# Two tiles' value products in one step, a fourth buffer for transposed weights, and earlier conversion of the values

## The chip, the core and the metric

The kernel runs on one core of one Trainium2 chip. What counts is the time of one execution on the device, in microseconds (us). Lower is better. A measurement of this kernel can tell a change of about 0.3% (3 us) from none.

The engines that matter here are TensorE (PE: matrix products, with its weight loads as PEld), VectorE (DVE), ScalarE (ACT), GpSimd (POOL) and SyncE (SP), whose queue issues most transfers. Each engine works through its own instructions in the order in which the program gives them.

## What is computed

The reference is causal attention with a cumulative bias, followed by two MLPs:

```python
scores = scale * np.matmul(q, k.transpose(0, 1, 3, 2))          # 4 batches, 8 heads, 576 tokens, 64 wide
cum = np.cumsum(np.maximum(s, 0.0), axis=-1)
bias = -(cum[:, :, :, None] - cum[:, :, None, :])
scores = np.where(causal, -1000000000.0, scores + np.minimum(bias, 0.0))
attn = np.exp(scores - np.max(scores, axis=-1, keepdims=True))
attn = attn / (np.sum(attn, axis=-1, keepdims=True) + 1e-09)
x = np.matmul(attn, v)                                          # then (2304 tokens, 512)
h = np.maximum(x @ w_in, 0.0);  x = h * h @ w_out               # first MLP, 2048 wide
h = x @ w_in2;                  y = (h * np.cos(h)) @ w_out2    # second MLP, 2048 wide
```

## The kernel before

The 2304 tokens are cut into nine blocks of 256. Attention is a list of 160 tiles ("jobs"): up to 128 query rows of one head against all keys up to the causal limit. The jobs of a block belong to eight heads of one or two batches, and a head has one or two jobs in a block. Jobs 0 to 31 (the first 16 head units, `n < EARLY`) are done in plain f32. From job 32 on, everything is split into a high and a low part.

`step` emits the program one step at a time, and this is what sets the order on every engine: there is one list of instructions, written step by step. Step i holds, for different jobs, the products of queries and keys (`emit_qk(i)`), the mask and the row minimum of job i - 1 on DVE (`emit_mask`), the exponential on ACT, and the split of job i - 2 into two f16 halves `p` on DVE (`emit_split`), after which SP issues a transposing transfer `pt<-p`. Then come the products with the values (`emit_pv`, "pv" below) of the job that is `lag` steps back: 3 for the early jobs, 5 for the others. One of these is a group of 9, 12 or 15 PE products of 64 columns in f16 (3 or 6 for the shortest tiles). When both heads of a pair are done, the next step evacuates them on DVE (`evacuate`, which writes `xp`), and PE turns `xp` by two f32 transposes into `xps` (`turn`).

Between these lie the slots of the first MLP for the block before: g1 (into `hps`, L844) and g2 (into `y`, L873), 12 products of 256 columns each, in f32r. `slots` is the list of all of them, and each step takes one or two. A block k takes J steps, from the step in which the attention of block k was done (`unit_done`) to the one in which that of block k + 1 is; the last of these J steps has no attention of its own. ACT makes three passes over each g1 result (`gact`: L855, L856, L857), and DVE one (L863).

The values are converted once for every pair of heads (16 conversions): `v_load` on POOL's queue, `v_square` on ACT, a sum over the partitions on PE (`v_sum`, L398), `v_scale` on DVE, `v_high` on ACT, `v_low` on DVE, `v_store` to `v_d` on SP. `vq` holds these by step, and `v_steps` sets the step of each conversion from V_TIME, V_NEAR and V_STRIDE. `load_v` reads a head's part back as `vb`.

The buffers that the change touches: `raw`, `hi` and `k2` (two of each) hold q and k of a head; `pt` has three buffers in turn; `p` has two (a third once the first MLP's weights are converted); `vt` has one and belongs to the conversion of values; all of the pool "at" share the same memory per partition.

After the first MLP come its remaining slots, and the second MLP (L1230 and L1285). The change leaves both alone.

Of the kernel before, what the change touches and what calls it, by code (L numbers as in the profile page):

```python
# [8 lines left out]
F32 = mybir.dt.float32  # L9
F32R = mybir.dt.float32r  # L10
F16 = mybir.dt.float16
# [3 lines left out]
ALU = mybir.AluOpType  # L15
# [9 lines left out]
BT = 256  # L25
# [8 lines left out]
LAG = (3, 5)  # L34
# [45 lines left out]
def _units():  # L80


    out = []
    for k, segs in enumerate(_segments()):
        for b, q0, rws, o in segs:
            nq = sum(rws)
            nk = q0 + nq
            out += [(k, b, h, q0, rws, o, nq, nk, max(nk, 256)) for h in range(H)]
    return out


KQ = 832

WAHEAD = 8
PROLOG_BITS = 0.75

EARLY = 16
# [10 lines left out]
XST_TO = 20  # L108
V_STRIDE = 11
V_NEAR = 6  # L110
V_TIME = 7


@with_exitstack
def attention_moe_moe_kernel(
# [18 lines left out]
    nc = tc.nc  # L134
    ctx.enter_context(tc.manual_schedule())
    heads = _units()

    dram = ctx.enter_context(tc.tile_pool(name="dram", bufs=1, space=DRAM))
    const = ctx.enter_context(tc.tile_pool(name="const", bufs=1))
# [5 lines left out]
    at = at_stack.enter_context(tc.tile_pool(name="at", bufs=1, side="right"))  # L145
# [5 lines left out]

    ext_d = dram.tile([len(heads), 4, KQ], F32, name="ext_d")
    c_d = dram.tile([B * H, 2, S], F32, name="c_d")
# [4 lines left out]
    ident = const.tile([128, 128], F32, name="ident")  # L158
    mask = const.tile([128, 640], BF16, name="mask")

    ones = const.tile([128, 128], F32, name="ones")
    yss = const.tile([128, 2 * NB1], F32, name="yss")
    vsc = const.tile([128, B * H], F32, name="vsc")
    hd, vd, vown = {}, {}, {}
# [29 lines left out]
    for x in range(H // 2):  # L194
        t = wp.tile([128, 2, 2 * BT], F32, tag=f"w{2 * NF - (2, 3, 4, 6)[x]}", name="early")
# [8 lines left out]
    def load_sums(x, eng):  # L204
        nc_ = c8[2 * x:2 * x + 2, 0:BT]
        eng.dma_start(out=early[x][64:65, :, BT:2 * BT], in_=nc_)
        eng.dma_start(out=early[x][65:66, :, 0:BT], in_=nc_)

    def load_raw(n):
        nq, nl = heads[n][6], heads[n][8]  # L210
        if n < H:
            return
        if n < EARLY:
            t = at.tile([128, KQ], F32, tag=("hi", "k2")[n % 2], bufs=2, name="early1")
            nc.sync.dma_start(out=t[0:64, 0:2 * BT], in_=qk[n, 0:64, 0:2 * BT])
            nc.sync.dma_start(out=t[64:66, 0:2 * BT], in_=c1_d[n - H])
            hd[n] = t
            return
        raw = at.tile([128, KQ], F32, tag="raw", bufs=2, name="raw")
        nc.sync.dma_start(out=raw[:, BT - nq:BT + nl], in_=qk[n, :, BT - nq:BT + nl])  # L220
        hd[n] = [None, None, raw]

    def v_own(b):
# [16 lines left out]
    vs = {}  # L240
# [12 lines left out]
    def store_ones(eng, n0, n1):  # L253

        for r in range(2):
            c = slice(BT * r, BT + (KQ - BT) * r)
            eng.dma_start(
# [6 lines left out]
        out=mask[:, 512:640], in_=mask[:, 512:640], pattern=[[-1, 128]], compare_op=ALU.is_ge,  # L264
# [4 lines left out]
        out=ident, in_=ident, pattern=[[-1, 128]], compare_op=ALU.not_equal, fill=1.0,  # L269
# [3 lines left out]
    for t in early[2:]:  # L273
        early_ones(t, nc.gpsimd)
    nc.vector.tensor_scalar(
        out=cs[0:32, 0:S], in0=cs[0:32, 0:S], scalar1=0.0, scalar2=8.0, op0=ALU.max, op1=ALU.mult
    )
    cc = []
    for x0, x1, t in ((0, BT, "xh"), (BT, S, "xl")):
        nc.vector.tensor_tensor_scan(  # L280
            out=c8[0:32, x0:x1], data0=cs[0:32, x0:x1], data1=cs[0:32, x0:x1],
# [5 lines left out]
    for r in range(2):  # L287
        nc.vector.memset(one[0:len(heads), BT * r:BT + (KQ - BT) * r], 1.0 - 2.0 * r)

# [19 lines left out]
    for x in range((XST + 1) // 2):  # L309
        t = wp.tile([128, 2, 512], F32, tag=f"w{2 * NF - 5 - x}", name="xst")  # L310
# [6 lines left out]
    jobs = []  # L317
    last_job = {}
    for n, (u, b, h, q0, rws, o, nq, nk, nl) in enumerate(heads):
        q = q0  # L320
# [12 lines left out]
    def load_ext(n):  # L333
        nq, nl = heads[n][6], heads[n][8]
        if n < EARLY:
            return
        hd[n][0] = at.tile([128, KQ], F32R, tag="hi", bufs=2, name="hi")
        hd[n][1] = at.tile([128, KQ], F32R, tag="k2", bufs=2, name="k2")
        nc.gpsimd.dma_start(out=hd[n][1][64:68, BT - nq:BT + nl], in_=ext_d[n, :, BT - nq:BT + nl])  # L339

    def prep_high(n):
        nq, nk = heads[n][6], heads[n][8]
        if n < EARLY:
            return
        hi, k2, raw = hd[n]
        nc.scalar.copy(hi[:, BT - nq:BT + nk], raw[:, BT - nq:BT + nk])
        nc.scalar.copy(k2[0:64, BT - nq:BT], raw[0:64, BT - nq:BT])

    def prep_low(n):
        nq, nk = heads[n][6], heads[n][8]  # L350
        if n < EARLY:
            return
        hi, k2, raw = hd[n]
        nc.vector.tensor_tensor(
            out=hi[64:128, BT - nq:BT], in0=raw[64:128, BT - nq:BT], in1=hi[64:128, BT - nq:BT], op=ALU.subtract
        )
        nc.vector.tensor_tensor(  # L357
            out=k2[0:64, BT:BT + nk], in0=raw[0:64, BT:BT + nk], in1=hi[0:64, BT:BT + nk], op=ALU.subtract
        )

    def load_v(n):
# [33 lines left out]
    def v_sum(g):  # L395
        n = g[2]
        vs[g]["ps"] = xps[:, BT:BT + n]
        nc.tensor.matmul(vs[g]["ps"], ones, vs[g]["ss"])  # L398

    def v_scale(g):  # L400
        b, h, n, nch = g
# [46 lines left out]
    def v_steps(gs, start):  # L448

        at, due = [], len(jobs) + V_TIME  # L450
        for b, h, n, nch in reversed(gs):
            first = next(
                i for i, j in enumerate(jobs) if j[0] >= 2 * H and heads[j[0]][1] == b and h <= heads[j[0]][2] < h + n
            )
            due = min(first - start + 3 - V_TIME, due - V_NEAR)
            at.insert(0, due)
# [6 lines left out]
    def v_add(gs, at, stored=True):  # L463

        for g, t in zip(gs, at):
            fs = []
            if g not in vs:
                fs, t = [(t, v_load)], t + 2
            fs += [(t, v_square), (t + 1, v_sum), (t + 2, v_scale), (t + 2, v_high), (t + 3, v_low)]
            for x, f in fs + [(t + 3, v_store)] * stored:  # L470
                vq.extend([] for _ in range(x + 1 - len(vq)))
                vq[x].append((f, g))

# [2 lines left out]
    def emit_qk(i):  # L476
        n, ti, q, r = jobs[i]
        u, b, h, q0, rws, o, nq, nk, nl = heads[n]
        if h % 2 == 0 and ti == 0:
            pd[n] = dict(z=at.tile([128, len(rws), 2], F32, tag="z", bufs=5, name="z", padded_shape=[128, 2, 2]))  # L480
        w = q + r
        segs = [(0, 288), (288, 288)] if w > 512 else [(0, max(w, 256))]
        qo = BT - nq + q - q0
        if n < EARLY:
            p = psa.tile([128, 512], F32, tag=f"qk{flip[0]}", bufs=1, name="qkp")
            flip[0] = (flip[0] + 1) % 3
            nc.tensor.matmul(p[0:r, 0:w], hd[n][0:66, qo:qo + r], hd[n][0:66, BT:BT + w])  # L487
            jd[i] = dict(ps=[(p, 0, w)], w=w)
            return
        hi, k2 = hd[n][0], hd[n][1]  # L490
        ps = []
        for k, (c0, cn) in enumerate(segs):
            p = psa.tile([128, 512], F32, tag=f"qk{flip[0]}", bufs=1, name="qkp")
            flip[0] = (flip[0] + 1) % 3
            for m, kk in ((hi, 128), (k2, 68)):
                nc.tensor.matmul(  # L496
                    p[0:r, 0:cn], m[0:kk, qo:qo + r], m[0:kk, BT + c0:BT + c0 + cn],
                    start=(kk == 128), stop=(kk == 68),
                )
            ps.append((p, c0, min(cn, w - c0)))  # L500
        jd[i] = dict(ps=ps, w=w)
# [16 lines left out]
    def p_tile(i):  # L518
        third = nw[2] >= 2 * NF and not wrest and i % 3 == 2
        return at.tile([128, 1280], F16, tag="p3" if third else "p", bufs=1 if third else 2, name="p")  # L520
# [19 lines left out]
    def emit_split(i):  # L540
        n, ti, q, r = jobs[i]
        j = jd[i]
        w, sb = j["w"], j["sb"]
        cw = 128 * ((w + 127) // 128)
        if n < EARLY:
            pp = j["ps"][0][0][:, BT:BT + cw]
            pt = at.tile([128, 640], F32, tag="pt", bufs=3, name="pt1")
            (nc.scalar.copy if ti else nc.vector.tensor_copy)(pt[:, 0:w], pp)
            j["pt"] = pt
            yield  # L550
            return
        p = p_tile(i)
        if cw > w:
            nc.gpsimd.memset(p[0:r, 0:2 * cw].rearrange("p (a c) -> p a c", a=2)[:, :, w:cw], 0.0)
        nc.vector.tensor_scalar(
            out=p[0:r, 0:w], in0=sb[0:r, 0:w], scalar1=PSC, scalar2=None, op0=ALU.mult
        )
        yield
        nc.vector.scalar_tensor_tensor(  # L559
            out=p[0:r, cw:cw + w], in0=sb[0:r, 0:w], scalar=PSC, in1=p[0:r, 0:w],  # L560
            op0=ALU.mult, op1=ALU.subtract,
        )
        pt = at.tile([128, 1280], F16, tag="pt", bufs=3, name="pt")
        pt = pt[:, 0:2 * cw // 128 * r].rearrange("p (a r) -> p a r", r=r)
        nc.sync.dma_start_transpose(out=pt, in_=p[0:r, 0:2 * cw])
        j["pt"] = pt
        yield
# [106 lines left out]
    def job(i):  # L674
        return jobs[i] if 0 <= i < NJ else None

    def lag(i):
        return LAG[not job(i) or jobs[i][0] >= EARLY]

    def heads_ahead(i, *fs):  # L680
        if job(i) and jobs[i][1] == 0:
# [301 lines left out]
    def step(moe=0, bits=0, attn=True):  # L983
# [49 lines left out]
        if attn:  # L1033
            heads_ahead(i, (nraw, load_raw, 4))
# [99 lines left out]
    while prog[0] < unit_done(0):  # L1134
        i = prog[0]
        x = i - FIRST_BITS
        step(bits=int((x + 1) * PROLOG_BITS) - int(x * PROLOG_BITS) if x >= 0 else 0)

    for k in range(NB1):
# [8 lines left out]
        for i in range(J):  # L1148
# [24 lines left out]
            n = len(slots) - last - nslots + math.ceil(nslots * (i + 1) / J)  # L1173
# [135 lines left out]
    for i in range(len(steps2) + G2LAG):  # L1309
# [6 lines left out]
        if new:  # L1316
            p, j, f = steps2[i]
# [89 lines left out]
```

## Time and profile before

| what | value |
|---|---|
| three runs | 998.5, 1000.96, 1001.49 us |
| median of them | 1000.96 us |
| the profiled execution's own time | 1003.76 us |
| its span, first to last instruction | 1002.0 us |
| busy, share of the span | PE 96%, PEld 74%, DVE 72%, ACT 65%, POOL 16% |
| chain that ended last | PE 79%, DVE 8%, DMA 6%, ACT 4% |
| mean granted TensorE clock | 0.995 |

The profiled execution is 2.8 us above the median of the three runs. Sums over the trace are made against 1003.76 us.

PE's busy share counts a product from its start to its modelled end, and products overlap, so 96% does not say that PE was at its best. The timeline does: the distance from one product's start to the next is what a product really costs there.

### The profile page before, as it was taken

Reading aid. Unit: us, or ns where it says so; the run is one execution under the profiler, and the core shown is the slowest. Engines: PE = TensorE matmul, PEld = TensorE weight load, DVE = VectorE, ACT = ScalarE, POOL = GpSimd, SP = SyncE. Lnnn points to the kernel's source line nnn. Section 1 sums busy time; section 2 is a strip of 40 time slices with the busy share of each in tenths; the row PEclk is TensorE's granted clock in tenths of the full one; section 3 lists DMA queues with packets and bytes.
Section 4 is the critical chain, followed back from the end, with each engine's and each line's share of the span. In section 5 each row is a group of like instructions: output and inputs, shape, how many; then the busy total and the mean of one; then the engine's idle time right before and its main releaser. Section 6 shows DMA issues by size and latency. Waiting matters only on the chain.

```text
span 1002.0 us, 20487 instructions
## 1 busy us (share of the span) xinstructions
PE 966.9 (96%) x7266; PEld 740.6 (74%) x7266; DVE 723.9 (72%) x1865; ACT 655.5 (65%) x1596; POOL 163.2 (16%) x258
## 2 busy tenths in 40 slices
PE   5999899999999999999999999999999999999998
PEld 4788898899999998999999997444544454444444
DVE  6879788867777897787888267798887545555555
ACT  4789777767777777767776578777766444433433
POOL 2000011111111121111211023330033341000000
PEclk9999999999999999999999999999999999999999
DMA  8955599746887986467898569210000000011001
GB/s 268 292 182 181 118 202 203 170 111 157 196 162 160 178 193 175 109 155 145 192 206 180 188 237 360 95 43 1 1 1 1 0 1 1 0 43 43 23 20 64
DMA packets 150711, 126.65 MB, mean 126 GB/s; under 512 B 108048, under 2 KB 125792, under 8 KB 150608
## 3 DMA queue, kind: packets, MB, share of 16 engines
q1 hardware_dynamic: 146688, 119.05, 46.1%
q0 software_dynamic: 3904, 6.29, 2.5%
q8 instruction: 57, 0.93, 0.4%
q14 instruction: 46, 0.38, 0.1%
q10 hardware_dynamic: 16, 0.01, 0.0%
HBM read 85.25 MB, written 15.81 MB: 101 GB/s over the span
## 4 chain that ended last, share of the span: by engine, by line
PE 79%; DVE 8%; DMA 6%; ACT 4%; issue 2%; SPq 1%; DVEq 0%; ACTq 0%
PE hps L844 18%; PE y L873 18%; PE o L1285 17%; PE hp L1230 17%; PE qkp L496 4%; PE pvs L590 4%; DMA rw<-in_w_dram 3%; DMA raw<-in_qk_dram 1%; PE xps L644 1%; DVE st L716 1%; DVE sb L510 1%; DVE gl L863 1%; DVE wt L737 0%; DVE k L357 0%; SPq L178 0%
## 5 line engine op out<-in xcount | busy, mean ns | idle before, releaser
L844 PE MATMUL hps<-xh,wt 128*128 128x256 f32 x1152 | 241.4, 292 | 4.1 <-ACT g L855 4.0
L873 PE MATMUL y<-gh,wt 128*128 128x256 f32 x1152 | 237.7, 289 | 0.0
L844 PEld LDWEIGHTS hps<-xh,wt 128*128 128x128 f32 x1152 | 191.7, 194 | 7.0 <-ACT g L855 5.5
L873 PEld LDWEIGHTS y<-gh,wt 128*128 128x128 f32 x1152 | 189.9, 192 | 1.3
L1230 PE MATMUL hp<-yh,wt 128*128 128x512 f16 (+1 forms) x640 | 185.9, 358 | 0.0
L1285 PE MATMUL o<-wt,gh 128*128 128x512 f16 x576 | 171.3, 379 | 2.0 <-ACT wt L1300 1.9
L873 PE MATMUL y<-gl,wt 128*128 128x256 f32 x576 | 163.4, 284 | 2.6 <-DVE gl L863 2.6
L844 PE MATMUL hps<-xl,wt 128*128 128x256 f32 x576 | 164.3, 285 | 0.9 <-DVE xl L661 0.9
L1230 PEld LDWEIGHTS <-wt 128*128 128x128 f16 x960 | 92.2, 98 | 93.3
L1242 ACT ACTIVATE a<-hp,hsc 128x512 f32<-128x512 f32 (+1 forms) x80 | 51.4, 643 | 118.6 <-PE hp L1230 117.2
L855 ACT ACTIVATE g<-hps 128x256 f32<-128x256 f32 x144 | 54.6, 379 | 107.7 <-PE hps L844 105.8
L1230 PE MATMUL hp<-yl,wt 128*128 128x512 f16 (+1 forms) x320 | 114.4, 358 | 0.0
L873 PEld LDWEIGHTS y<-gl,wt 128*128 128x128 f32 x576 | 110.6, 192 | 3.7 <-DVE gl L863 3.1
L844 PEld LDWEIGHTS hps<-xl,wt 128*128 128x128 f32 x576 | 111.7, 194 | 1.4 <-DVE xl L661 1.1
L1285 PE MATMUL o<-wt,gl 128*128 128x512 f16 x288 | 109.2, 379 | 0.4 <-DVE gl L1272 0.4
L1243 DVE TENSOR_SCALAR kf<-a 128x512 f32<-128x512 f32 (+1 forms) x80 | 34.5, 431 | 103.8 <-ACT a L1242 103.4
L1285 PEld LDWEIGHTS <-gh 128*128 128x128 f16 x576 | 56.2, 98 | 66.7 <-issue 2.4
L527 ACT ACTIVATE sb<-sb,nb 128x128 f32<-128x128 f32 (+8 forms) x160 | 93.7, 586 | 12.1 <-DVE nb L510 12.0
L339 POOL DMA_DIRECT2D k<-ext_d x80 | 40.8, 510 | 341.9 <-ACT g L856 92.3
L510 DVE CUSTOM_DVE_ANT_0 sb<-qkp,mask 128x128 f32<-128x128 f32 (+8 forms) x160 | 72.7, 454 | 13.8 <-PE qkp L487 8.6
L1251 ACT ACTIVATE a<-kf 128x512 f32<-128x512 f32 (+1 forms) x80 | 46.8, 585 | 46.6 <-DVE kf L1244 46.1
L559 DVE SCALAR_TENSOR_TENSOR p<-sb,p 128x512 f16<-128x512 f32 (+7 forms) x128 | 72.4, 565 | 4.0
(119 smaller groups left out, 1680.1 us busy)
## 6 DMA issues: line engine op xcount, KB each, us to landing
rw<-in_w_dram SPq DMA_DIRECT2D x64, 512.0 KB
raw<-in_qk_dram SPq DMA_DIRECT2D x32, 352.0 KB
raw<-in_qk_dram SPq DMA_DIRECT2D x16, 384.0 KB
v_d<-vt SPq DMA_DIRECT2D x16, 320.0 KB
raw<-in_qk_dram SPq DMA_DIRECT2D x16, 320.0 KB
vb<-v_d SPq DMA_DIRECT2D x32, 160.0 KB
vr<-in_v_dram POOLq DMA_DIRECT2D x15, 320.0 KB, 4.7
y_d<-yst SPq DMA_DIRECT2D x18, 256.0 KB
```

The lines of the kernel that those rows point to most:

```text
L339: nc.gpsimd.dma_start(out=hd[n][1][64:68, BT - nq:BT + nl], in_=ext_d[n, :, BT - nq:BT + nl])
L496: nc.tensor.matmul(p[0:r, 0:cn], m[0:kk, qo:qo + r], m[0:kk, BT + c0:BT + c0 + cn], start=(kk == 128), stop=(kk == 68),)
L510: nc.vector.tensor_tensor_reduce(out=sb[0:r, c0:c0 + cn], in0=p[0:r, 0:cn], in1=mask[0:r, mo + c0:mo + c0 + cn], scale=-0.125, scalar=(3.0 ...
L527: nc.scalar.activation(out=sb[0:r, 0:w], in_=sb[0:r, 0:w], func=ACTF.Exp, scale=-1.0, bias=j["nb"], accum_out=pd[n - h % 2]["z"][0:r, ti, ...
L559: nc.vector.scalar_tensor_tensor(out=p[0:r, cw:cw + w], in0=sb[0:r, 0:w], scalar=PSC, in1=p[0:r, 0:w], op0=ALU.mult, op1=ALU.subtract,)
L844: nc.tensor.matmul(hp, w[:, a, c * 128:(c + 1) * 128], (xh, xl)[e][:, c, :], start=(n == 0), stop=(n == 3 * KD - 1),)
L855: nc.scalar.activation(out=g, in_=hp, func=ACTF.Relu)
L873: nc.tensor.matmul(yps[k][d // 2][:, d % 2, :], w[:, a, d * 128:(d + 1) * 128], (gh, gl)[e], start=(f == 0 and n == 0 and d % 2 == 0), sto ...
L1230: nc.tensor.matmul(hp, w[:, a, c * 128:(c + 1) * 128], (yh, yl)[e][:, c, :], start=(m == 0), stop=(m == 3 * KD - 1),)
L1242: nc.scalar.activation(out=a, in_=hp, func=ACTF.Copy, scale=sm["hsc"][:, j, f:f + 1], bias=0.25)
L1251: nc.scalar.activation(out=a, in_=kf, func=ACTF.Sin, scale=-6.2831850)
L1285: nc.tensor.matmul(ops[j][a], (gh, gl)[e][:, a * 128:(a + 1) * 128], w[:, x, :], start=(first and m == 0), stop=(last and m == 2),)
```

## The change

In the late part of attention (jobs from 32 on), `lag` becomes 4 for every odd job and stays 5 for every even one. An even job j and the odd job j + 1 then both have their products with the values in step j + 5, and the steps between have none. `unit_done` takes the odd job's lag, so it comes one step earlier for every block from 2 on.

A job whose number is 3 modulo 4 takes its transposed weights into a buffer of its own: `pt4` (1024 columns), or, where it needs more, the buffer of `vt`. The other three of each four jobs share the three `pt` buffers as before.

Memory for `pt4` comes from `raw`, `hi`, `k2` and the early heads' tiles, which have 768 columns in place of 832 (`qb(n)` is where the keys start: 256, or 192 for a head with 576 keys), and from `ones`, which is one column and is broadcast where it is used.

V_TIME goes from 7 to 10, so each conversion of values starts up to three steps sooner; inside a conversion, the sum on PE and all that follows it come one step later than they did after the squares.

```diff
-V_TIME = 7
+V_TIME = 10
...
-    ones = const.tile([128, 128], F32, name="ones")
+    ones = const.tile([128, 1], F32, name="ones")
...
+    def qb(n):
+        return min(BT, SQ - heads[n][8])
...
-        raw = at.tile([128, KQ], F32, tag="raw", bufs=2, name="raw")
-        nc.sync.dma_start(out=raw[:, BT - nq:BT + nl], in_=qk[n, :, BT - nq:BT + nl])
+        raw = at.tile([128, SQ], F32, tag="raw", bufs=2, name="raw")
+        nc.sync.dma_start(out=raw[:, qb(n) - nq:qb(n) + nl], in_=qk[n, :, BT - nq:BT + nl])
...
-        nc.tensor.matmul(vs[g]["ps"], ones, vs[g]["ss"])
+        nc.tensor.matmul(vs[g]["ps"], ones.to_broadcast([128, 128]), vs[g]["ss"])
...
-            fs += [(t, v_square), (t + 1, v_sum), (t + 2, v_scale), (t + 2, v_high), (t + 3, v_low)]
-            for x, f in fs + [(t + 3, v_store)] * stored:
+            fs += [(t, v_square), (t + 2, v_sum), (t + 3, v_scale), (t + 3, v_high), (t + 4, v_low)]
+            for x, f in fs + [(t + 4, v_store)] * stored:
...
-        pt = at.tile([128, 1280], F16, tag="pt", bufs=3, name="pt")
+        if i % 4 < 3:
+            pt = at.tile([128, 1280], F16, tag="pt", bufs=3, name="pt")
+        elif cw * r <= 512 * 128:
+            pt = at.tile([128, 1024], F16, tag="pt4", bufs=1, name="pt4")
+        else:
+            pt = at.tile([128, 1280], F16, tag="vt", bufs=1, name="pt5")
...
     def lag(i):
-        return LAG[not job(i) or jobs[i][0] >= EARLY]
+        if job(i) and jobs[i][0] < EARLY:
+            return LAG[0]
+        return LAG[1] - (i % 2 if job(i) else 0)
```

The lines of the changed kernel lie up to 11 further down than those before (L590 is L599 there, L844 is L855, L873 is L884, L398 is L402, L565 is L574).

PE at the first place where a fourth buffer is used, jobs 34 and 35. The rows before, from the last of the nine products of job 34 on:

```order
L590 LDWEIGHTS pt_1472
L590 MATMUL pvs_78<-vb_1501,pt_1472 128x64
L873 MATMUL y0_1627<-gh_1547,wt_318 128x256
L873 MATMUL y0_1627<-gl_1615,wt_318 128x256
L873 MATMUL y0_1627<-gh_1547,wt_318 128x256 x2
```

The same place after the change:

```order
L599 LDWEIGHTS pt_1479
L599 MATMUL pvs_78<-vb_1508,pt_1479 128x64
L599 LDWEIGHTS pt4_1551
L599 MATMUL pvs_78<-vb_1508,pt4_1551 128x64
L599 LDWEIGHTS pt4_1551
```

The twelve products of job 35 now follow those of job 34 directly; before, a whole g2, the products of queries and keys and a g1 lay between them. Over the late part PE's list has 128 groups of pv before and 64 after. Of the late turns, 36 stood directly behind a pv group before and 5 by themselves; after, none stands behind a group and 41 stand between slots. Of the sums of the values (L398), 1 late one stood by itself and 5 do now.

PE at the end of the first block, in the step without attention between steps 36 and 37. The rows before, from the end of a g2 to the start of the next g1:

```order
L873 MATMUL y_646<-gh,wt 128x256 x2
L873 MATMUL y_646<-gl,wt 128x256
L873 MATMUL y_646<-gh,wt 128x256
L398 MATMUL xps<-ss,ones 128x2
L844 MATMUL hps<-xh,wt 128x256
L844 MATMUL hps<-xl,wt 128x256
```

After the change that g2 is followed by the g1 directly, and the sum of the same conversion stands two steps earlier, behind the turn in step 35:

```order
L855 MATMUL hps<-xl,wt 128x256
L855 MATMUL hps<-xh,wt 128x256
L653 MATMUL xps<-ident,xp 128x128 x2
L402 MATMUL xps<-ss,ones 128x2
L884 MATMUL y_645<-gh,wt 128x256
L884 MATMUL y_645<-gl,wt 128x256
```

SP's queue around the first use of the fourth buffer, with what each row waits for. Before:

```order
L565 DMA_TRANSPOSE pt<-p 128x6x128 [waits DVE_49,PE_49]
L367 DMA vb<-v_d 128x512
L220 DMA raw<-in_qk_dram 128x768 [waits DMAHW0_49,DVE_49,Activation_49]
L565 DMA_TRANSPOSE pt<-p 128x8x128 [waits DMAHW1_49,DMAHW2_49,DVE_49,PE_49]
L882 DMA y_d<-yst 128x512 [waits Activation_49]
```

After:

```order
L574 DMA_TRANSPOSE pt<-p 128x6x128 [waits DVE_49,PE_49]
L371 DMA vb<-v_d 128x512
L224 DMA raw<-in_qk_dram 128x768 [waits DMAHW0_49,DMAHW1_49,DVE_49,Activation_49]
L436 DMA v_d<-vt 128x2x640 [waits DVE_49]
L574 DMA_TRANSPOSE pt_1551<-p 128x8x128 [waits DMAHW2_49,DVE_49]
L893 DMA y_d<-yst 128x512 [waits Activation_49]
```

The store of the third conversion of values has moved ahead of this transfer, and the transfer no longer has a wait for PE here. Later uses wait for the products of the job four back, where the rows before wait for the job three back.

## Rows read from the trace of the kernel before

**Rows 1.** Whom PE waited for, 115 to 560 us: in total, times, longest.

```profile
PE hps L844 <- ACT g L855: 3.2, 4, 1.4
PE pvs L590 <- DVE xp L630: 2.5, 2, 1.4
```

**Rows 2.** Two stretches: us, each engine's busy time (count), granted clock, DMA share, GB/s.

```profile
118.20:121.50 3.30, 3.30 (x15) 3.11 (x15) 1.18 (x4) 0.66 (x2) 0.00 (x0) 0.50 0.08 30
255.00:376.00 121.00, 121.00 (x1216) 117.98 (x1216) 96.61 (x266) 91.64 (x247) 17.85 (x42) 1.00 0.83 178
```

**Rows 3.** Timeline of PE, nine products with values: start us, us, what.

```profile
301.78 0.28 PE L844 MATMUL hps<-xh,wt 128*128 128x256 f32 x1
301.90 0.43 PE L590 MATMUL pvs<-vb,pt 128*128 128x64 f16 x9
...
302.38 0.28 PE L873 MATMUL y<-gl,wt 128*128 128x256 f32 x1
```

**Rows 4.** Timeline of PE, twelve products with values.

```profile
305.35 0.28 PE L844 MATMUL hps<-xh,wt 128*128 128x256 f32 x1
305.48 0.52 PE L590 MATMUL pvs<-vb,pt 128*128 128x64 f16 x12
...
306.04 0.28 PE L873 MATMUL y<-gl,wt 128*128 128x256 f32 x1
```

**Rows 5.** Timeline of PE, six products of a tile of 64 rows.

```profile
237.92 0.28 PE L873 MATMUL y<-gh,wt 128*128 128x256 f32 x1
238.13 0.38 PE L590 MATMUL pvs<-vb,pt 128*64 128x64 f16 x6
...
238.66 0.28 PE L844 MATMUL hps<-xl,wt 128*128 128x256 f32 x1
```

**Rows 6.** Timeline of PE, fifteen products of a tile of 64 rows.

```profile
188.98 0.28 PE L873 MATMUL y<-gh,wt 128*128 128x256 f32 x1
189.19 0.66 PE L590 MATMUL pvs<-vb,pt 128*64 128x64 f16 x15
...
190.00 0.28 PE L844 MATMUL hps<-xl,wt 128*128 128x256 f32 x1
```

**Rows 7.** Timeline of PE, fifteen products of a full tile and a turn.

```profile
517.21 0.28 PE L873 MATMUL y<-gh,wt 128*128 128x256 f32 x1
517.34 0.61 PE L590 MATMUL pvs<-vb,pt 128*128 128x64 f16 x15
517.78 0.31 PE L644 MATMUL xps<-ident,xp 128*128 128x128 f32 x1
...
518.05 0.28 PE L844 MATMUL hps<-xl,wt 128*128 128x256 f32 x1
```

**Rows 8.** Timeline of PE, a turn by itself.

```profile
505.76 0.28 PE L873 MATMUL y<-gh,wt 128*128 128x256 f32 x1
505.88 0.33 PE L644 MATMUL xps<-ident,xp 128*128 128x128 f32 x1
...
506.17 0.28 PE L844 MATMUL hps<-xl,wt 128*128 128x256 f32 x1
```

**Rows 9.** Timeline of PE, the sum of the third conversion; in brackets the idle time before.

```profile
115.92 0.28 PE L873 MATMUL y<-gh,wt 128*128 128x256 f32 x1
117.74 0.38 PE L398 MATMUL xps<-ss,ones 128*128 128x2 f32 x2 [1.55 <-ACT vt L390]
```

**Rows 10.** Whom SP's queue waited for, whole span.

```profile
SPq L565 <- PE pvs L590: 81.5, 71, 3.9
```

**Rows 11.** Whom ACT waited for, whole span.

```profile
ACT hi L346 <- DMA raw<-in_qk_dram: 14.0, 9, 4.3
```

**Rows 12.** Timeline of DVE, SP and PE around job 129.

```profile
435.38 0.62 DVE L559 SCALAR_TENSOR_TENSOR p<-sb,p 128x448 f16<-128x448 f32 x1
...
436.49 1.23 SPq L565 DMA_TRANSPOSE pt<-p  x1
...
440.77 0.44 PE L590 MATMUL pvs<-vb,pt 128*128 128x64 f16 x9
```

More of the change, by code (lines that the diff above doesn't have):

```diff
@@ L92 @@
 KQ = 832
+SQ = 768
 WAHEAD = 8
@@ L213, in load_raw @@
         if n < EARLY:
-            t = at.tile([128, KQ], F32, tag=("hi", "k2")[n % 2], bufs=2, name="early1")
+            t = at.tile([128, SQ], F32, tag=("hi", "k2")[n % 2], bufs=2, name="early1")
             nc.sync.dma_start(out=t[0:64, 0:2 * BT], in_=qk[n, 0:64, 0:2 * BT])
@@ L336, in load_ext @@
             return
-        hd[n][0] = at.tile([128, KQ], F32R, tag="hi", bufs=2, name="hi")
-        hd[n][1] = at.tile([128, KQ], F32R, tag="k2", bufs=2, name="k2")
-        nc.gpsimd.dma_start(out=hd[n][1][64:68, BT - nq:BT + nl], in_=ext_d[n, :, BT - nq:BT + nl])
+        hd[n][0] = at.tile([128, SQ], F32R, tag="hi", bufs=2, name="hi")
+        hd[n][1] = at.tile([128, SQ], F32R, tag="k2", bufs=2, name="k2")
+        nc.gpsimd.dma_start(out=hd[n][1][64:68, qb(n) - nq:qb(n) + nl], in_=ext_d[n, :, BT - nq:BT + nl])
     def prep_high(n):
@@ L345, in prep_high @@
         hi, k2, raw = hd[n]
-        nc.scalar.copy(hi[:, BT - nq:BT + nk], raw[:, BT - nq:BT + nk])
-        nc.scalar.copy(k2[0:64, BT - nq:BT], raw[0:64, BT - nq:BT])
+        nc.scalar.copy(hi[:, qb(n) - nq:qb(n) + nk], raw[:, qb(n) - nq:qb(n) + nk])
+        nc.scalar.copy(k2[0:64, qb(n) - nq:qb(n)], raw[0:64, qb(n) - nq:qb(n)])
     def prep_low(n):
@@ L354, in prep_low @@
         nc.vector.tensor_tensor(
-            out=hi[64:128, BT - nq:BT], in0=raw[64:128, BT - nq:BT], in1=hi[64:128, BT - nq:BT], op=ALU.subtract
+            out=hi[64:128, qb(n) - nq:qb(n)], in0=raw[64:128, qb(n) - nq:qb(n)], in1=hi[64:128, qb(n) - nq:qb(n)], op=ALU.subtract
         )
         nc.vector.tensor_tensor(
-            out=k2[0:64, BT:BT + nk], in0=raw[0:64, BT:BT + nk], in1=hi[0:64, BT:BT + nk], op=ALU.subtract
+            out=k2[0:64, qb(n):qb(n) + nk], in0=raw[0:64, qb(n):qb(n) + nk], in1=hi[0:64, qb(n):qb(n) + nk], op=ALU.subtract
         )
@@ L482, in emit_qk @@
         segs = [(0, 288), (288, 288)] if w > 512 else [(0, max(w, 256))]
-        qo = BT - nq + q - q0
+        qo = qb(n) - nq + q - q0
         if n < EARLY:
@@ L496, in emit_qk @@
                 nc.tensor.matmul(
-                    p[0:r, 0:cn], m[0:kk, qo:qo + r], m[0:kk, BT + c0:BT + c0 + cn],
+                    p[0:r, 0:cn], m[0:kk, qo:qo + r], m[0:kk, qb(n) + c0:qb(n) + c0 + cn],
                     start=(kk == 128), stop=(kk == 68),
```

## The prediction

> **What bounds the kernel now.** I read the busy time by stages first. Between 255 and 376 us, PE is busy for all of 121 us while DVE has 96.6 and ACT 91.6 of it [rows 2]. So over most of the late part of attention PE sets the pace, and the other engines have a fifth of the time to spare. The second view is the list of what PE waited for between 115 and 560 us. The two longest entries are 3.2 us for ACT's first pass over a g1 result and 2.5 us for evacuations [rows 1]. Almost nothing is there to be won by removing waits in general, so the question is what PE's own sequence costs.
>
> For that I read PE's timeline row by row and take distances from start to start. Inside g1 and g2, one product starts 0.12 us after the other. From the last product of a g1 to the second product of the next g2 would therefore be 0.24 us. With nine products with values in between it is 302.38 - 301.78 = 0.60 us [rows 3], so the group costs 0.36. With twelve it is 306.04 - 305.35 = 0.69, so 0.45 [rows 4]. Three more products cost 0.09: 0.03 each (0.029 with the third digit). What is left for the group as such is 0.36 - 9 x 0.029 = **0.09 us**, paid once for leaving f32r products and coming back.
>
> A tile of 64 rows pays more. Six products cost 238.66 - 237.92 - 0.24 = 0.50 [rows 5], fifteen cost 190.00 - 188.98 - 0.24 = 0.78 [rows 6]. By the formula of full tiles they would cost 0.27 and 0.53. The excess is 0.23 and 0.25, nearly the same for six and for fifteen, so it too belongs to the group and not to the product.
>
> **The change, part by part.**
>
> Grouping. The number of products with values stays; 128 groups become 64. Each merger saves one fixed cost: 64 x 0.093 = -6.0 us. Eight of the mergers join two tiles of 64 rows (two blocks have heads with only such a tile), and each saves the excess of about 0.24 once more: -1.9 us. Where a full tile's three products are followed by six of a 64-row tile, the excess stays, and I count the plain cost alone. Bounds: zero, if the cost is paid whenever a new buffer is loaded, and -6.0 - 24 x 0.24 = -11.8, if those mixed pairs (16 of them) save the excess too. I take -7.9, since the rows show a fixed part.
>
> Turns and sums standing alone. A turn behind a group costs little: 518.05 - 517.21 - 0.24 = 0.60 for fifteen products and a turn [rows 7], of which the formula gives 0.53 to the products, so 0.07. By itself a turn costs 506.17 - 505.76 - 0.24 = 0.17 [rows 8]. It pays the trip out of f32r itself. 36 more turns and 4 more sums stand alone after the change: 40 x 0.10 = +4.0 us. So PE's sequence gains 7.9 - 4.0 = 3.9 us net, half of what the halving of groups suggests.
>
> The Trainium skill speaks against even this. "TensorEngine Tiling (Array Packing)", section "Instruction Overhead", says that each matmul has an overhead of about 60 cycles, however few columns it has; then the cost would lie in the 64-column product itself, and putting groups together would save nothing. As an estimate by that page of the Trainium skill, the grouping gives 0 and the sum below loses 7.9. Rows 3 and 4 show both parts side by side: 0.029 per product, and 0.09 that nine and twelve products share.
>
> The sum of the third conversion. At 115.92 PE starts the last product of a g2 and could start the next thing at 116.04, but the sum starts at 117.74: 1.55 us of its wait are for ACT's squares, which were issued just ahead of it [rows 9]. After the change this sum stands two steps earlier, behind a turn, and its squares were issued two steps before it. The wait of 1.7 us goes. Right after it PE's granted clock is 0.50 from 118.20 to 121.50, which is the lower level, 1.2 GHz; PE had just stood still for those 1.7 us. In this stretch DVE is busy for 1.18 us and ACT for 0.66 of 3.30 [rows 2], so PE was the one that others waited for, and running it at half speed cost about 1.65 us. Without the wait the clock likely stays up. Next in PE's queue is a g1 whose buffer ACT has freed, so I see no new wait in its place. Bounds: 0, if DVE or ACT holds PE there anyway, and -3.35. I take -3.0.
>
> Waits for evacuations (2.5 us in two places [rows 1]). Both lie where the last g2 of a block has been done and DVE copies `y` out before it can evacuate a pair: the group of pv behind it waits. After the change the pair is evacuated in the same relation to that g2, and the turn takes the group's place in the wait. I count 0. Bounds: 0 and -2.5, with another 1.65 if a fall of the clock goes with it.
>
> SP's queue. The transfers `pt<-p` waited for PE 71 times, 81.5 us in all [rows 10], with the loads of `raw` and `vb` queued behind them. With a ring of four, the buffer's last user is one step further back, so these waits shrink. The path gets little of it: ACT waited 14.0 us for `raw` [rows 11], and PE's waits of 3.2 us for ACT [rows 1] are what came through of that. Bounds 0 and -3.2; `raw` gains under a microsecond per load against its whole journey, so I take -0.7.
>
> Earlier conversions. No work is added. But one more conversion comes before 115 us, where ACT and DVE do more per step than later. PE waits for ACT there in places. Taking the price of one wait of [rows 9] as the upper bound, the cost is 0 to +1.7; I take +0.5. POOL's queue now gets the next load of values right behind the DVE pass that frees its buffer, with the next step's `k2` rows and the zeroing of `p` behind it; these have a step of slack.
>
> The rest at nothing. 768 columns in place of 832 move the same bytes. The buffer of `vt` is taken by four tiles only (147, 151, 155, 159), long after the last conversion, and each waits for the one four jobs back. A one-column `ones` is read 128 times for the stationary side of 16 sums; nothing in the trace prices that, and I bound it by 0 and one more fixed cost each, +1.5.
>
> Sum: -7.9 + 4.0 - 3.0 + 0 - 0.7 + 0.5 = **-7.1 us**, from 1003.76 us to 996.7. The median of the runs lies 2.8 us below the profiled one; from there it is 1000.96 - 7.1, **994 us**.
>
> **The rivals.**
>
> The odd tile's transfer is late (slower). An odd job's products come one step sooner. Take job 129: its weights are ready at 435.38 + 0.62 = 436.0, and after the change it would be wanted with job 128, at 440.8 [rows 12]. That leaves 4.8 us for queueing, 1.2 us of issue and the journey; this is the shortest lead that I find, in the stretches of short steps, which hold 24 odd jobs. Before, the transfer's own wait and the extra step left its lead larger. When it lands is not in the trace. The rival needs journeys of over 3.6 us; each microsecond above that, over 24 jobs, costs 24 us. To end slower by 3 us it must eat 7.1 + 3, which is 0.42 us on each of the 24. At that point the time is 1004; a fall of the clock beside it would make it 1006.
>
> The group's cost is not saved (no change): it is paid with each product's or each buffer's first weight load and not at the change of format. Then -7.9 falls away and the lone turns still cost 4.0: +4.0 - 3.0 - 0.7 + 0.5 = +0.8, so 1002. If half of it is saved, it is -3.1, at 998. By the rule of the Trainium skill's page named above, this is what happens. For it speaks only that the rows never show two tiles side by side. The same result comes if DVE, which now evacuates and prepares q and k in the same step, holds up the lone turns.
>
> More goes than I count (faster still). If the evacuation waits and their fall of the clock go as well, another 2.5 + 1.65 come off: 990.
>
> **How the numbers follow.** My forecast has 0.55: 994, with 991.5 to 997.5 as its own range. More gain has 0.13, at 990. The group's cost not saved, in whole or half, has 0.20, 998 to 1002. The late transfer has 0.12, at 1004 to 1006. The range that leaves out the late transfer and the slow end of the third is 989.5 to 1001. A measurement tells 0.3%, so faster means below 998: the forecast and the greater gain, 0.68. The third rival is mostly the same: 0.19. Slower has the late transfer and a little of the third: 0.13.
>
> **What would show it.** In the changed profile, 21 or 24 products with values should stand in one row, and the distance around 21 of them should be 0.24 + 0.09 + 21 x 0.029 = 0.94 us. A lone turn of two should cost about 0.1 more than one behind a group. The row for the sum waiting for ACT's squares should be gone, and the stretch behind it at full clock. SP's wait for PE should be a small part of 81.5 us. The evacuation waits should stand at the turn (L653), not at pv. What would make me wrong: PE's pv group waiting for `pt` with nothing on the engines late, or a new fall of the granted clock between 200 and 560 us.

## The result, and the profile after

The changed kernel takes 1011.96 us (median of six runs, 1005.76 to 1017.37), the kernel before 1001.01 us: the ratio is 1.011 with a 95% interval of 1.0071 to 1.0149. It is slower by about 11 us; 994 was forecast, and the slowest of the rivals ended at 1006.

The profiled execution of the changed kernel took 1014.2 us. Its cores view gives span and mean granted clock (before: 1002.0 us and 0.995):

```profile
core 0: 1012.4 us, clock 0.988
```

A span times one minus its clock is what half speed cost in it, as far as PE had work to do. Over the runs on record the median clock is 0.990 after and 0.998 before, so 10.1 us against 2.0: up to 8 of the 11 us are the lower clock, and the rest is PE standing still or working longer.

Whom PE waited for, 115 to 560 us, beside [rows 1]:

```profile
PE pvs L599 <- DMA vb<-v_d: 3.2, 1, 3.2
PE xps L653 <- DVE xp L639: 2.8, 3, 1.1
PE qkp L500 <- DMA k<-ext_d: 2.4, 2, 1.5
PE qkp L500 <- DVE nb L514: 2.3, 3, 1.1
```

ACT's first pass over g1 is gone from this list, and the evacuation (`xp`) is now waited for by the turn. New are two transfers, `vb` and the rows `k<-ext_d`, which POOL loads into `k2`. The longest wait lies ahead of this stretch. The timelines of ACT, PE, POOL and SP at that place, an instruction's start and length, and in brackets the idle time before it:

```profile
79.07 0.64 SPq L436 DMA_DIRECT2D v_d<-vt  x1
...
79.18 0.76 POOL L383 DMA_DIRECT2D vr<-in_v_dram  x1 [73.10 <-ACT st L717]
...
88.37 0.47 ACT L394 ACTIVATE vt<-vr 128x320 f16<-128x320 f32 x1 [9.37 <-DMA v_d<-vt]
...
90.71 0.69 PE L542 MATMUL qkp<-ident,sb 128*128 128x128 f32 x2 [8.97 <-ACT sb L531]
```

The store of the first conversion and the load of the second go out 0.1 us apart. The second's squares are already next in ACT's queue; they read `vr` and write `vt`, so they need both transfers landed, and ACT stands for 9.37 us. The exponential behind them is what PE needs: PE stands for 8.97. The load took 8.0 us to land, at 87.16; in the kernel before it took from 75.77 to 79.14. It went out among five loads of first-MLP weights (`rw`, 512 KB each, 77.1 to 80.8 us), and from 84 to 88 us the DMA engines were busy throughout (405 GB/s).

The second place is the products of an odd tile, job 111, and its transfers on SP:

```profile
395.99 0.37 SPq L436 DMA_DIRECT2D v_d<-vt  x1
396.47 0.41 SPq L224 DMA_DIRECT2D raw<-in_qk_dram  x1
397.55 1.94 SPq L574 DMA_TRANSPOSE pt<-p  x1
399.53 0.57 SPq L371 DMA_DIRECT2D vb<-v_d  x1
...
404.21 0.96 PE L599 MATMUL pvs<-vb,pt 128*64 128x64 f16 x15 [3.23 <-DMA vb<-v_d]
```

The windows view of the two stretches of half clock that go with them, and of the stretch of [rows 2] (us, busy time of PE, PEld, DVE, ACT, POOL, granted clock, DMA share, GB/s):

```profile
86.00:99.65 13.65, 8.94 (x41) 8.76 (x42) 8.16 (x22) 9.98 (x27) 0.00 (x0) 0.50 0.33 133
403.50:413.74 10.24, 9.53 (x53) 9.12 (x53) 4.30 (x21) 2.66 (x10) 0.92 (x3) 0.50 0.30 73
255.00:376.00 121.00, 119.57 (x1207) 117.34 (x1206) 96.65 (x267) 93.12 (x250) 17.73 (x41) 1.00 0.80 179
```

In the first two the clock is at 0.50, the lower level of 1.2 GHz; PE had stopped before each fall, and went on at half speed for 9 us after each wait. The second is what the prediction had named as a sign that it was wrong, a new fall between 200 and 560 us. Between the starts of g1's 97th and 145th product the changed kernel loses 11.6 us against the trace of before; between the 961st and the 1057th, 7.1. From the 97th to the 1393rd product outside these two it gains 9.3, of which some 3.4 (an estimate: half of two falls of 3.41 us each, at 118 [rows 2] and at 197 us) are only the falls of the clock in the profiled execution of before. From there to the last product of g2 it loses 1.5 again.

The grouping itself does what was forecast. PE's timeline around 21 products, then around a turn by itself:

```profile
301.03 0.28 PE L855 MATMUL hps<-xh,wt 128*128 128x256 f32 x1
301.15 0.79 PE L599 MATMUL pvs<-vb,pt 128*128 128x64 f16 x21
...
301.98 0.28 PE L884 MATMUL y<-gl,wt 128*128 128x256 f32 x1
```

```profile
269.43 0.28 PE L884 MATMUL y<-gh,wt 128*128 128x256 f32 x1
269.55 0.38 PE L653 MATMUL xps<-ident,xp 128*128 128x128 f32 x2
...
269.89 0.28 PE L855 MATMUL hps<-xl,wt 128*128 128x256 f32 x1
```

21 products take 301.98 - 301.03 - 0.24 = 0.71 us, where nine and twelve apart take 0.36 + 0.45 = 0.81 [rows 3, 4]. Two tiles of 64 rows together, 30 products, take 1.26 in the trace of experiment 2 (369.6 us), where two of them apart take 2 x 0.78 [rows 6].

### The profile page after: what moved, and what is told of

The parts are those of the page before. It is cut to its first block, busy times and chain, and to the rows that moved or that the text cites. A ratio compares the mean times of both kernels' runs of the same rounds, so it can differ in the third digit from the quotient of the medians.

```text
span 1012.4 us, 20487 instructions
## 1 busy us (share of the span) xinstructions
PE 965.2 (95%) x7266; PEld 743.2 (73%) x7266; DVE 721.7 (71%) x1865; ACT 654.8 (65%) x1596; POOL 162.7 (16%) x258
## 4 chain that ended last, share of the span: by engine, by line
PE 43%; DVE 4%; ACT 2%; issue 1%; DVEq 0%; ACTq 0%
PE o L1296 17%; PE hp L1241 16%; PE hps L855 4%; PE y L884 4%; PE qkp L500 1%; PE pvs L599 1%; ACT wt L742 0%; DVE kf L1255 0%; DVE wt L751 0%; DVE a L1268 0%; DVE k L361 0%; DVE wsc L781 0%; DVE kf L1254 0%; ACT a L1253 0%; ACT a L1262 0%
## 5 line engine op out<-in xcount | busy, mean ns | idle before, releaser
L855 PE MATMUL hps<-xh,wt 128*128 128x256 f32 x1152 | 241.6, 292 | 0.9 <-ACT g L866 0.8
L884 PE MATMUL y<-gh,wt 128*128 128x256 f32 x1152 | 238.2, 290 | 0.0
L855 PEld LDWEIGHTS hps<-xh,wt 128*128 128x128 f32 x1152 | 193.0, 195 | 3.2 <-ACT g L866 1.8
L884 PEld LDWEIGHTS y<-gh,wt 128*128 128x128 f32 x1152 | 190.5, 192 | 1.3
L884 PE MATMUL y<-gl,wt 128*128 128x256 f32 x576 | 164.0, 285 | 2.7 <-DVE gl L874 2.7
L855 PE MATMUL hps<-xl,wt 128*128 128x256 f32 x576 | 165.0, 286 | 0.7 <-DVE xl L670 0.7
L884 PEld LDWEIGHTS y<-gl,wt 128*128 128x128 f32 x576 | 110.9, 193 | 3.6 <-DVE gl L874 3.1
L855 PEld LDWEIGHTS hps<-xl,wt 128*128 128x128 f32 x576 | 112.3, 195 | 1.3 <-DVE xl L670 0.9
L874 DVE TENSOR_TENSOR gl<-g,gh 128x256 fp32r<-128x256 f32 x144 | 61.1, 425 | 20.0 <-PE y L884 10.0
```

What stands on the lines that cost most here:

```text
L855: nc.tensor.matmul(hp, w[:, a, c * 128:(c + 1) * 128], (xh, xl)[e][:, c, :], start=(n == 0), stop=(n == 3 * KD - 1),)
L874: nc.vector.tensor_tensor(out=gl, in0=g, in1=gh, op=ALU.subtract)
L884: nc.tensor.matmul(yps[k][d // 2][:, d % 2, :], w[:, a, d * 128:(d + 1) * 128], (gh, gl)[e], start=(f == 0 and n == 0 and d % 2 == 0), sto ...
```

## The experiments

All times are medians; the ratio is against the kernel before, run on the same chip beside them. "Spacing" below stands for the first edit.

**1. Conversions at least six steps apart** (`e1_spacing`), on the changed kernel:

```diff
-            at[x] = max(0, min(due, free))
+            at[x] = max(at[x - 1] + V_NEAR if x else 0, min(due, free))
```

> The changed kernel, with one rule added: a conversion of values starts at least six steps behind the one before it (the second one starts in step 27 in place of 25, the next seven move two steps likewise). Theory A (the slowdown is the second conversion: its squares stand in ACT's queue for a load that is issued in the step in which the first conversion's low parts are made; the changed kernel's trace shows ACT waiting 9.4 us there and 13.65 us of half clock behind it): that wait is gone, PE has no stall over 3 us between 75 and 95 us, and 1012 - 9 - 6.8 = 996 us, between 992 and 1002. Theory B (the grouped products, the lone turns and the bunched work of DVE and ACT cost the time, and the wait at 88 us lies mostly beside work that would be late anyway): 1008 or more.

Measured: 1011.4 us, 1.0104 (1.0081 to 1.0126). The wait at 90 us shrank from 9 to 2.8 us, but the time did not move: theory A falls as the whole story. From the 97th to the 145th product of g1 it takes 19.3 us in place of 29.1, and from there to the 961st 284.4 in place of 274.8: other waits have grown in its place. The timelines of POOL, DVE and PE show one:

```profile
159.54 0.20 POOL L558 MEMSET p<- 64x128 f16 x1
...
164.50 1.00 DVE L429 SCALAR_TENSOR_TENSOR vt<-vr,vsc,vt 128x320 f16<-128x320 f32 x2
...
166.08 0.74 POOL L383 DMA_DIRECT2D vr<-in_v_dram  x1 [6.34 <-issue]
166.90 0.52 POOL L343 DMA_DIRECT2D k<-ext_d  x1
...
172.96 0.47 PE L500 MATMUL qkp<-k 68*64 68x288 f32 x1 [4.11 <-DMA k<-ext_d]
```

POOL stood 6.34 us ahead of the load. The profile names no releaser ("issue"), but the load overwrites `vr`, which DVE's low parts (L429) of the conversion before still read in the same step. The `k` rows stood behind it, went out at 166.90, landed at 172.82, and PE waited 4.11 us for them. The median journey of such rows in this trace is 3.3 us, so these were late twice: on POOL's queue, and on their way behind the load.

**2. Grouping alone** (`e2_group_only`): V_TIME 7, and the conversion's steps as before.

```diff
-V_TIME = 10
+V_TIME = 7
...
-            fs += [(t, v_square), (t + 2, v_sum), (t + 3, v_scale), (t + 3, v_high), (t + 4, v_low)]
-            for x, f in fs + [(t + 4, v_store)] * stored:
+            fs += [(t, v_square), (t + 1, v_sum), (t + 2, v_scale), (t + 2, v_high), (t + 3, v_low)]
+            for x, f in fs + [(t + 3, v_store)] * stored:
```

> The changed kernel with the conversions of values as they were (V_TIME 7, sum, scale and low parts one, two and three steps behind the squares). What stays is the grouping, the fourth buffer and the 768 columns. Theory A: no stall between 75 and 95 us, the sum of the third conversion waits again for ACT's squares (1.7 us); the grouping gives 3.9 to 8 us, so 993 to 997, or up to 1003 if the load of vb for an odd tile comes late as at 404 us in the changed kernel (3.4 us and 10.2 us of half clock there). Theory B: 1006 or more.

Measured: 1001.28 us, 1.0007 (0.9995 to 1.0019). No harm, so theory B falls; but no gain either. PE's waits in this kernel, 115 to 560 us:

```profile
PE xps L653 <- DVE xp L639: 2.7, 3, 1.1
PE xps L402 <- ACT vt L394: 2.5, 4, 1.6
PE pvs L599 <- DMA vb<-v_d: 2.1, 2, 1.1
PE hps L855 <- ACT g L866: 1.7, 2, 1.2
```

**3. The conversions alone** (`e3_conversion_only`), on the kernel before:

```diff
-V_TIME = 7
+V_TIME = 10
...
+            fs += [(t, v_square), (t + 2, v_sum), (t + 3, v_scale), (t + 3, v_high), (t + 4, v_low)]
```

> The kernel before with the new conversion alone (V_TIME 10, sum, scale and low parts two, three and four steps behind the squares), without grouping, with three buffers pt and 832 columns. Theory A: ACT waits some 9 us for the second load of values, with a fall of the clock behind it: 1001 - 3 + 15.8 = 1014, between 1008 and 1017. Theory B: the conversions alone do no harm, 996 to 1002.

Measured: 1014.28 us, 1.0134 (1.0112 to 1.0156), as theory A has it. PE waited 8.70 us at 91.75 and 3.83 us at 378.61, where the `k` rows, which POOL had issued behind a wait of 7.0 us, landed at 378.48 (the profile names DVE's pass over `k`, which ended at the same moment). The loss belongs to the conversions.

**4. Spacing, and the odd single tile's `vb` one step sooner** (`e4_spacing_vb_sooner`):

```diff
-            for j in stage(0, i - 2):
+            for j in stage(0, i - 2 + bool(i % 2 == 0 and job(i - 1) and jobs[i - 1][0] >= EARLY)):
```

> As the kernel with the conversions at least six steps apart, and the load of vb for an odd tile that is its head's only one is issued one step sooner, together with that of the even tile before it. Theory C (the stall of 3.4 us at 404 us and the 10.2 us of half clock behind it are due to the odd tile's values, which are wanted one step earlier than before): 3 to 8 us less than with the spacing alone, no wait of pv for vb over 1 us, no fall of the clock between 380 and 420 us. Rival (that stall is chance, from whatever the DMA engines carried in this execution, or the transposed weights pt are as late): the same time as with the spacing alone, within 2 us, or a wait for pt in its place.

Measured: 1012.31 us, 1.0116 (1.0093 to 1.0139): no gain over the first. PE's products with values now wait 6.7 us for `pt` instead of 5.8 for `vb`: whatever of the odd tile is issued last is late.

From these four came theory D: the longer conversion makes its low parts in the very step in which the next load is issued, so POOL stands still with the `k` rows behind it.

**5. Spacing and the old length, sooner start kept** (`e5_old_length`): the first edit, and the conversion's steps of the second without its V_TIME.

```diff
+            at[x] = max(at[x - 1] + V_NEAR if x else 0, min(due, free))
...
+            fs += [(t, v_square), (t + 1, v_sum), (t + 2, v_scale), (t + 2, v_high), (t + 3, v_low)]
```

> The changed kernel with conversions at least six steps apart (as in the first experiment, 1011.4 us) and with the old length of a conversion: the sum, scale and low parts one, two and three steps behind the squares, so that the low parts and the store come one step before the next load. V_TIME stays 10: they still start sooner than before. Theory D (what costs the time is that the load of the next values is issued in the step in which the low parts of the last are made and stored: POOL stands 6.5 us for DVE with the rows k<-ext_d behind it, and a store and a load of 320 KB each go out together, with the transfers pt and vb behind them): no wait of PE for k<-ext_d, none of pv over 2 us, and 998 to 1003 us, as with the grouping alone (1001.3). Theory E (the sooner start is what costs: three steps' worth of DVE and ACT work where the steps are full): 1007 to 1012.

Measured: 1000.31 us, 0.9988 (0.9975 to 1.0002). Theory D, not E: with the added step gone, the loss is gone. It does not clear the sooner start altogether. The first conversion starts in step 21 in every kernel, so with six steps between them the second to the ninth start one step sooner than in the kernel before, and the last seven three steps; old length with the full three steps was not run, and in experiment 10 the last two are put back. POOL's wait at the 13 loads after 115 us, in this order from the kernel before, the first experiment and the sixth (least, median, greatest ns):

```profile
L379 POOLq EVENT_SEMAPHORE  x13: 17/2926/6797, 122.1 to 387.3; - x13
```

```profile
L383 POOLq EVENT_SEMAPHORE  x13: 17/6446/8279, 119.1 to 387.2; - x13
```

```profile
L383 POOLq EVENT_SEMAPHORE  x13: 17/2348/6873, 120.1 to 379.2; - x13
```

**6. Spacing, new length, each load one step later** (`e6_load_later`):

```diff
-                fs, t = [(t, v_load)], t + 2
+                fs, t = [(t + 1, v_load)], t + 2
```

> As the first experiment (new length, at least six steps apart, 1011.4 us), but each load of values is issued one step later, one step before its squares instead of two. Theory D: the load no longer meets the store nor waits on POOL for the low parts; 995 to 1002 us, if one step is enough for the load (5.9 us from issue to landing in the first experiment's trace); where it is not, ACT waits for vr by a microsecond or two at a time. Theory E, and the theory that the added step between squares and low parts harms by itself: 1007 or more, with no wait on POOL.

Measured: 1005.67 us, 1.0046 (1.0026 to 1.0065), between both forecasts: 5.7 us of the loss gone with POOL's added wait, and no wait of PE for `k<-ext_d` left. What remains is the odd tile: pv waited 3.12 us for `vb` at 394.21, with 10.2 us of half clock.

**7. The same, and `vb` one step sooner** (`e7_load_later_vb_sooner`), with the first edit:

```diff
+                fs, t = [(t + 1, v_load)], t + 2
...
+            for j in stage(0, i - 2 + bool(i % 2 == 0 and job(i - 1) and jobs[i - 1][0] >= EARLY)):
```

> As the kernel with each load of values one step later, and the odd single tile's vb one step sooner as well. With the store and the load apart, theory D says that the shorter lead of the odd tile costs little: 0 to 2 us less than without it. Theory C (the odd tile's vb is late by itself): 3 to 8 us less than without it.

Measured: 1001.55 us, 1.0008 (0.9991 to 1.0025), 4.1 us less. With POOL out of the way the sooner `vb` helps, as theory C says; but in the trace job 111 still waits, now for `pt`. SP and PE:

```profile
386.76 0.38 SPq L436 DMA_DIRECT2D v_d<-vt  x1
387.23 0.42 SPq L224 DMA_DIRECT2D raw<-in_qk_dram  x1
387.76 3.91 SPq L574 DMA_TRANSPOSE pt<-p  x2
...
394.45 0.66 PE L599 MATMUL pvs<-vb,pt 128*64 128x64 f16 x15 [3.14 <-DMA pt<-p]
```

A store of 320 KB, a load of as much on POOL (386.9 us) and `raw` go out within half a microsecond, just ahead of job 111's transfer.

**8. The conversions alone, spaced, each load one step later** (`e8_conversion_load_later`), on the kernel before, with the first edit and the third, no grouping:

```diff
+V_TIME = 10
...
+                fs, t = [(t + 1, v_load)], t + 2
```

> The kernel before with the new conversions alone (1014.3 us), at least six steps apart and each load one step later; no grouping. Theory D: the 14 us go, 996 to 1002; below 1000 if the wait of the sum for ACT's squares, which the longer conversion removes, is worth what I gave it. Theory E: 1008 to 1014.

Measured: 1002.73 us, 1.0022 (1.0005 to 1.004). Nearly all of the 14 us of experiment 3 are gone, so theory D holds without grouping too (two edits at once; the first of them alone gave nothing on the changed kernel). The wait of the third sum is gone as well, and yet nothing is won. PE waits longer for ACT near the second conversion, where the three waits of this kind add up to 4.2 us against 2.2 before:

```profile
91.47 0.44 PE L538 MATMUL qkp<-ident,sb 128*128 128x128 f32 x2 [2.98 <-ACT sb L527]
```

**9. Spacing, and loads issued by SP behind the store** (`e9_load_on_sp`):

```diff
-        eng = nc.sync if g[:2] == (V_ORDER[0], 0) else nc.gpsimd
+        eng = nc.sync
```

> As the first experiment (new length, at least six steps apart, 1011.4 us), but the loads of values are issued by SP right behind the store, for which SP waits anyway, in place of POOL. Loads and stores go out together as before; POOL no longer waits for the low parts. If POOL's standing still is one of the two causes, PE's waits for k<-ext_d at 173 and 376 us (5.5 us together) go with the fall of the clock behind the first, and what stays is the odd tile's wait at about 400 us: 1003 to 1007. If not POOL's wait but the meeting of store and load on the DMA engines makes those rows late, k<-ext_d still waits and the time stays at 1009 to 1013.

Measured: 1003.43 us, 1.002 (1.0 to 1.004). Store and load still go out together, and the waits for `k<-ext_d` are gone: it was their place behind POOL's load that made those rows late. How much of it was POOL standing still, and how much the load ahead of them on its way, this run does not part. Waits for `vb` stay, 4.7 us.

**10. As 7, the last two conversions three steps later** (`e10_last_two_later`):

```diff
+        for x in (14, 15):
+            at[x] += 3
```

> As the kernel with loads one step later and the odd tile's vb one step sooner (1001.55 us; its trace has pv waiting 3.1 us for pt of job 111 at 394 us, with 6.8 us of half clock behind it), but the last two conversions start three steps later. The store and load of 320 KB each no longer go out just ahead of job 111's transfer. If that meeting, in the stretch of short steps at a block's end, is what is left of the loss, the wait at 394 us goes: 996 to 999 us. If the odd tile is late there whatever else is on the DMA engines, the wait stays, 1000 to 1003.

Measured: 998.88 us, 0.9976 (0.9962 to 0.9989). The wait at 394 us is gone. Three steps later is where these two started in the kernel before (steps 114 and 120), so for them the sooner start did cost something: 2.7 us against experiment 7.

**11. Grouping alone, `vb` one step sooner** (`e11_group_vb_sooner`), with the second edit:

```diff
+            for j in stage(0, i - 2 + bool(i % 2 == 0 and job(i - 1) and jobs[i - 1][0] >= EARLY)):
```

> The grouping with the conversions as they were before (1001.3 us), and the odd single tile's vb one step sooner. Two waits of pv for vb, 2.1 us together at about 202 us, should go: 998 to 1000 us. If the odd tile's pt is as late as its vb, they become waits for pt and the time stays at 1000 to 1002.

Measured: 1000.18 us, 0.9993 (0.9982 to 1.0004). The time does not tell the two apart, the trace does: the waits for `vb` (2.1 us) became waits for `pt` (3.1), the second of them.

**12. Spacing, old length, `vb` sooner, the last two later** (`e12_old_length_vb_last_two`), with the edits of the fifth and:

```diff
+        for x in (14, 15):
+            at[x] += 3
...
+            for j in stage(0, i - 2 + bool(i % 2 == 0 and job(i - 1) and jobs[i - 1][0] >= EARLY)):
```

> The kernel with conversions of the old length, six steps apart and started sooner (1000.3 us; its trace has one wait of 1.6 us for vb at 393 us with 3.4 us of half clock), plus the odd single tile's vb one step sooner and the last two conversions three steps later. If the odd tile's lead is what holds it at 1000, 996 to 998.5 us, better than the kernel before by 0.3% or so. If the waits of ACT and of turns behind q.k products that came with grouping and sooner conversions are what is left, 999 to 1001.

Measured: 997.28 us, 0.9969 (0.9955 to 0.9983): the fastest, and faster than the kernel before by 3 us. Its clock stayed up in the profiled execution:

```profile
core 0: 995.7 us, clock 1.000
```

## Why the prediction was wrong

**The step that failed** is the one on earlier conversions: "the cost is 0 to +1.7; I take +0.5", and with it "these have a step of slack", said of the `k` rows behind POOL's load. Alone, the conversions cost 13 to 14 us (experiment 3). I had counted that no work is added, and had seen that POOL's load would stand right behind DVE's pass; not what the added step does to a buffer's turn-over. The low parts now come six steps behind the load, and the next load comes six steps on, or four between the first conversion, which cannot start before step 21, and the second. Then everyone who needs `vr` or `vt` next waits inside one step, on queues with other work behind: ACT at 88 us, POOL from then on. There was no step of slack: POOL's median wait went from 2.9 to 6.4 us, and PE stood for the rows behind it. Giving the step back (5) or issuing the loads a step later (8) takes away all but 0 to 2 us of it; with grouping the later loads leave 4.4 (6), most of it the odd tile's.

**The slower rival** (0.12) was right in kind. It does not reach 1012, but with POOL's wait repaired, experiment 6 lies at 1005.7, where the rival had put it. The odd tile's transfers are late in the short steps, and a fall of the clock goes with it. From experiment 6 to 10 they give 6.8 us, most of it clock: over the runs, span times one minus clock is 8.2 us on average in 6 and 3.3 in 10. Two things were off: the late transfer was first `vb`, which I had not counted at all (a head with only one tile loads it on its own, behind the transposing transfer), and the loss was not spread over 24 jobs but stood at one or two places, mostly where the store and load of a conversion go out just ahead.

**Grouping.** -0.093 for each merger: 0.81 - 0.71 = 0.10 measured (0.09 with the third digit); a pair of 64-row tiles saves 1.56 - 1.26 = 0.30, where 0.33 was counted. The Trainium skill's rule ("TensorEngine Tiling (Array Packing)", section "Instruction Overhead"), taken as a cost of each product by which nothing is saved, does not show here. **Lone turns** I priced too high: a turn of two alone takes 269.89 - 269.43 - 0.24 = 0.22, and behind nine products 0.527 - 0.354 = 0.17 in the trace of before, so 0.05 and not the 0.10 that I took from a single turn [rows 8]. From the 577th to the 913th product of g1, with 14 mergers, seven turns and a sum alone, grouping alone takes 104.0 us against 105.4: -1.4, where these prices give -0.9. Why grouping alone still measures as no change (2): what PE's sequence gained went into waits. From the 97th product of g1 to the last of g2 the profiled execution takes 538.3 us, and that of before 541.7 with some 3.4 of lower clock in it; PE's waits there add up to 17.8 us against 14.4. So the sequence is about 3.4 us shorter, near the 3.9 forecast, though its parts, at the prices above, would have given more. New are the waits for `vb` (2.1 us), and those of sums for squares grew from 1.55 to 2.5. How much each gives back was not tried apart. Over the runs the clock takes 3.4 us on average, against 1.6 before.

**The third conversion's sum.** The wait went, as forecast. But the term of -3.0 had two faults. Its half about the clock was taken off twice: the falls in the profiled execution are not in most runs (median clock 0.998 against 0.995, 3.0 us over the span), and going from 1003.76 to the median had already taken off 2.8. And its other half came back elsewhere: experiment 8 has this gain, without grouping, and is not faster.

**What held.** SP's transfers waited for PE's products with values 9.5 us in place of 81.5 [rows 10]; ACT's wait for `raw` fell from 14.0 to 6.6 [rows 11], and PE's wait for ACT's first pass went; evacuations are waited for at the turn, 2.8 us. The time that SP's transfers stand did not go with it: they now wait for DVE's second half of `p`, 135.4 us where it was 45.8. Whom SP and ACT waited for, whole span, the changed kernel, with the kernel before in the third line:

```profile
SPq L574 <- PE pvs L599: 9.5, 10, 1.7
SPq L574 <- DVE p L563: 135.4, 98, 5.7
SPq L565 <- DVE p L559: 45.8, 49, 3.6
ACT hi L350 <- DMA raw<-in_qk_dram: 6.6, 5, 2.3
```

With the conversions repaired, experiment 12 is 3 us faster than the kernel before. That this is near the 3.9 that I had for PE's sequence is in part luck: it holds two edits that the change did not have (the sooner `vb` and the last two conversions put back), and no run parts what each term of the sum gave. Over the runs, the clock takes 1.3 us on average in it and 2.1 before, so some 0.8 of the gain is the clock.

## What to carry to other kernels

When a step is added between a buffer's load and its last use, look up the next owner's load in the order: if it now falls into the same step, the queue that issues it stops there, and what stands behind it pays, though no work was added. When two consumers are put together, list every transfer of the one that comes sooner, not the one that was in view. And a stall in a profiled execution that a clock fall follows must not be taken off both from that execution and on the way to the median.

## What was not expected of the hardware

A wait can cost more than itself. After PE stood for 3.2 us at 404, the clock stayed at 0.50 until 413.74, 9.5 us of work at half speed. It does not always follow: in experiment 8 PE stood for 2.98 us at 91.47 and the clock was at 1.00 to the end of the second MLP. The falls differ from run to run, and so the changed kernel's six runs spread over 11.6 us and those of the kernel before, in the same measurement, over 4.7.

A transposing transfer's issue on SP does not always take as long: the median is 1.2 us in every trace, but it took 1.94 for job 111 in the changed kernel, 2.06 at 163.35 in experiment 1, and 2.38 at 197.1 in the kernel before; the transfers behind it on SP start later by as much. What lengthens it was not tried.
